# Units 22 and 23 of a top-k attention plus MLP kernel: transposed on TensorE and weighed one step sooner

## The chip, the core and the metric

The kernel runs on one NeuronCore of one Trainium2 chip, in one launch. The metric is device time in microseconds. Three runs of the kernel before took 1432.84, 1432.95 and 1433.07 us, so its median is 1432.95 us. A further execution was taken with the hardware profiler, and all rows below come from it.

## The reference

An attention over the 32 best keys of each query is followed by a two-layer perceptron with a leaky ReLU. All inputs are float32.

```python
B, H, S, D = 8, 8, 576, 64
scores = (q @ k.transpose(0, 1, 3, 2)) / sqrt(D)
kth = np.partition(scores, -32, axis=-1)[..., -32:-31]
scores = np.where(scores >= kth, scores, -1e9)
attn = exp(scores - max(scores)); attn /= sum(attn) + 1e-9
x = (attn @ v).transpose(0, 2, 1, 3).reshape(4608, 512)
h = x @ w_in                      # 512 -> 2048
out = np.maximum(0.01 * h, h) @ w_out   # 2048 -> 512
```

## The kernel before, in words

**Units and steps.** Heads are taken two at a time. A unit is 128 score rows for each of two heads, that is a block of 128 queries of one pair of heads, or the two 64-query remainders of two pairs. There are 144 units, and the kernel works on one unit per step. Steps come in pairs, written out by hand in `even(s)` (L729) and `odd(s, ...)` (L781); the order of the instructions on every engine is the order of this text, and each engine runs its own queue strictly in that order. In step s three units are in work: `cur` is unit s, `old` is unit s-1, `older` is unit s-2.

**The path of one unit.**

- The scores come from TensorE (`scores`, L237) into PSUM tiles `wide` and `narrow`, for two units at a time at the end of an even step; ScalarE copies them to `s_sb` (L246) in the odd step that follows. The tag `wide` has two buffers.
- In its own step, VectorE finds the 32 largest of each row (`top_k`): two TENSOR_TENSOR on the two halves of the row (L270), then rounds of MAX8 (L276) and MATCH_REPLACE8 (L281).
- One step later, ScalarE takes the negated limit (`limits`, L291), masks (L297), takes exponents with their sums (L300) and adds the small constant (L305, tile `ze`). GpSimd prepares the bias of the exponent (L292, L293).
- VectorE takes the reciprocal of `ze` (L309, tile `rz`). This happens only in even steps: for `older` after the two L270, and for `old` ahead of the last two MAX8. ScalarE then normalizes (L312).
- The weights must be turned before they can be multiplied with the values. The usual way is `split` and `transpose`: GpSimd copies the high and the low 16 bits apart (L321, two copies), SyncE writes them to DRAM (L322, two DMAs) and then starts a transposing DMA that brings them back as `wT` (L326).
- TensorE multiplies `wT` with the values (`weigh_whole`, L365) into a `wide` tile, and ScalarE copies the product to `x` (`keep_values`, L388).

**The hasty way.** Units 142 and 143, the last two, go another way. `transpose_in_haste` (L328) turns the nine 128-column blocks of `s_sb` with nine TensorE transposes (L336), into two `wide` tiles; `keep_transposed` (L339) copies these to `wT` on ScalarE with two copies (L342, 1024 and 128 columns). No GpSimd copy and no DMA is used. In the even step the two L342 stand after the exponents of `old`. In the odd step, L800 to L807 put these in a row: the transposes of `older`, the exponents of `old`, the two L342, and then at once the weighing of both units and its L388.

```python
    HASTY = (142, 143)                                  # L635
    def values_at(n):                                   # step in which unit n is weighed
        return (n | 1) + (2 if n in HASTY else 3)
```

**The MLP between the steps.** Tokens are cut in chunks: four of 128 tokens (chunks 0 to 3, `plain`), then sixteen of 256 (chunks 4 to 19, the rest of `mlp`). A chunk becomes ready when its last unit is weighed (`attended`, L654, in odd steps), and the MLP is a generator, of which `mlp_steps(budget)` runs a few matmuls at seven places of each step. For the big chunks `slot_budget` (L660) spreads the work of a chunk over the steps up to the next one's readiness; during the small chunks the budget is `EARLY_SHARE`, times 0.6 in a step whose `older` is hasty. The MLP's first layer is 8 groups of 8 matmuls (L504); `keep_hidden` (L492) then applies the leaky ReLU on ScalarE, one instruction for each group. This instruction is not written at once: it goes to a list `due`, and `catch_up` writes it at the next of a few fixed places, one of which lies between the masks of `old` and the normalization of `older` in every even step. The second layer is L518 (and L596 for the small chunks), its output is copied by L526 (or L588).

**Sums on GpSimd.** The second layer of the big chunks uses sums of weights and of hidden parts, which GpSimd makes with TENSOR_TENSOR (L443). They wait in a list, and `sum_now(2)` writes two of them in an even step, `sum_now(3)` three in an odd one. The generator of chunk 4 adds two sums of `w_out` (128x1024) of its own when it starts (`sum_last_weights`, L466).

**Which units end chunk 4.** Units 16 to 19 are the 64-query remainders of batches 0 and 1, units 20 to 23 the first whole blocks of batch 1; the last tokens of chunk 4 come from units 22 and 23.

Of the kernel before, what the change touches and what calls it, by code (L numbers as in the profile page):

```python
# [20 lines left out]
def kernel(  # L21
# [241 lines left out]
    def top_k(u):  # L263

        u.tops = small.tile([P, 2, ROUNDS, 8], F32, name="tops")
        pairs = work.tile([P, 2, 2, HS], F32, name="pairs", bufs=1)
        for n, op in enumerate((ALU.max, ALU.min)):
            nc.vector.tensor_tensor(pairs[:, :, n, :], u.both[:, :, 0:HS], u.both[:, :, HS:S], op)  # L270
        yield
        for r in range(ROUNDS):
            rest = [pairs[:, i, 0, :] if r < ROUNDS // 2 else
                    pairs[:, i, :, :].rearrange("p n h -> p (n h)") for i in range(2)]
            for i in range(2):
                nc.vector.max(out=u.tops[:, i, r, :], in_=rest[i])  # L276
            if r == ROUNDS - 2:
                yield
            if r + 1 < ROUNDS:
                for i in range(2):  # L280
                    nc.vector.match_replace(out=rest[i], in_to_replace=u.tops[:, i, r, :],  # L281
                                            in_values=rest[i], imm_value=LOWEST)
            yield
# [348 lines left out]

    HASTY = (142, 143)  # L635

    def values_at(n):

        return (n | 1) + (2 if n in HASTY else 3)

    steps = units

    def unit(n):
        return steps[n] if FIRST <= n < len(steps) else None
# [15 lines left out]
    def slot_budget(s):  # L660

        after = [at for at, _ in ready_at if at > s]
        if len(after) >= len(CHUNKS) - EARLY:
            return EARLY_SHARE * (0.6 if s - 2 in HASTY else 1.0)
        until = after[0] if after else s + 1
# [7 lines left out]
    with tc.manual_schedule():  # L673
# [55 lines left out]
        def even(s):  # L729
            cur, old, older = unit(s), unit(s - 1), unit(s - 2)  # L730
            in_haste = s - 2 in HASTY
            new = [u for u in steps[s + 2:s + 4] if u]
# [48 lines left out]
        def odd(s, new, ps, weighed):  # L781
            cur, old, older = unit(s), unit(s - 1), unit(s - 2)
            in_haste = s - 2 in HASTY
            picks = top_k(cur) if cur else iter(())
# [210 lines left out]
```

## Time and profile before

| what | value |
| --- | --- |
| median of the runs | 1432.95 us (1432.84 to 1433.07) |
| profiled execution, its own time | 1433.87 us |
| its span, first to last instruction | 1431.8 us |
| TensorE matmul busy | 1347.2 us, 94% |
| VectorE busy | 1319.2 us, 92% |
| ScalarE busy | 1023.0 us, 71% |
| GpSimd busy | 709.8 us, 50% |
| TensorE clock, mean of what was granted | 0.979 |

Shares over the whole span hide the stages: a stage is read from its own window. "PEclk" is the granted TensorE clock, 1.00 being full speed. In a timeline row the columns are the start, the duration of the row's instructions together, the engine, the line, the operation, output and input tiles, shapes, the count, and in brackets the idle time ahead of it with what ended it. Every float32 matmul shows as two rows' worth of instructions, so "x16" of L504 is eight matmuls. In step order, VectorE's L270 mark where steps begin: 287.98 us (step 24), 297.80 (25), 306.58 (26), 315.45 (27), 324.23 (28), 333.10 (29).

### The profile page before, as it was taken

How to read it: one execution, taken by the hardware profiler on the slowest of the kernel's cores; microseconds unless marked ns; L12 is line 12 of the kernel's file. 1: busy time of each engine (PE TensorE's matmuls, PEld its weight loads, DVE VectorE, ACT ScalarE, POOL GpSimd, SP SyncE). 2: the span in 40 equal slices, each digit the busy share in tenths (PEclk: the TensorE clock that was granted, in tenths of full speed). 3: DMA queues.
4: the chain of work that ended last, by engine and by line, in shares of the span. 5: the costliest groups of instructions: out<-in, count | busy, mean ns of one | idle time of the engine just before them, and what ended most of it. 6: DMA issues, size and time to landing. Idle time of an engine off the chain costs nothing.

```text
span 1431.8 us, 27705 instructions
## 1 busy us (share of the span) xinstructions
PE 1347.2 (94%) x9794; PEld 1031.4 (72%) x9794; DVE 1319.2 (92%) x3412; ACT 1023.0 (71%) x2144; POOL 709.8 (50%) x796
## 2 busy tenths in 40 slices
PE   6679599969999999999999999999999999999998
PEld 2234354447778888878888888888878888888887
DVE  7989999899999999999999999999999999999700
ACT  6866767677777777777777777777777777777621
POOL 2332373335555555555555555555555555555512
PEclk9889899989999999999999999999999999999999
DMA  7772545655666556756666556655676565655400
GB/s 291 250 222 67 140 134 172 193 141 133 165 185 174 144 144 186 196 152 139 177 175 173 141 164 174 186 142 155 175 182 168 141 157 142 169 145 136 125 12 15
DMA packets 399388, 224.91 MB, mean 157 GB/s; under 512 B 339216, under 2 KB 348432, under 8 KB 397328
## 3 DMA queue, kind: packets, MB, share of 16 engines
q1 hardware_dynamic: 398096, 222.08, 56.9%
q8 instruction: 77, 1.26, 0.4%
q10 hardware_dynamic: 1152, 1.05, 0.2%
q14 instruction: 63, 0.52, 0.1%
HBM read 46.14 MB, written 93.19 MB: 97 GB/s over the span
## 4 chain that ended last, share of the span: by engine, by line
DVE 70%; PE 18%; issue 6%; ACT 4%; DMA 1%; POOL 0%; DVEq 0%; POOLq 0%; ACTq 0%
DVE tops L276 34%; DVE pairs L281 26%; DVE pairs L270 7%; PE ph L504 4%; PE pz L518 4%; PE ph L405 3%; PE pz L596 2%; PE wide L365 2%; DMA raw<-in_weights_dram 1%; DVE rz L309 1%; PE wide L237 1%; ACT s_sb L300 1%; ACT s_sb L312 1%; DVE w_in L158 1%; PE narrow L237 0%
## 5 line engine op out<-in xcount | busy, mean ns | idle before, releaser
L276 DVE MAX8 tops<-pairs 128x8 f32<-128x288 f32 (+1 forms) x1152 | 636.3, 592 | 0.3 <-DVE rz L309 0.3
L504 PE MATMUL ph<-x,w_in 128*128 128x256 f32 x2048 | 457.5, 382 | 4.7 <-ACT gT L492 4.4
L281 DVE MATCH_REPLACE8 pairs<-tops,pairs 128x288 f32<-128x288 f32 (+1 forms) x864 | 460.6, 539 | 0.0
L504 PEld LDWEIGHTS ph<-x,w_in 128*128 128x128 f32 x2048 | 384.3, 190 | 84.0 <-issue 16.5
L321 POOL COPY split<-s_sb 128x1152 uint16<-128x1152 uint16 x284 | 316.8, 1144 | 186.1 <-ACT s_sb L312 186.1
L312 ACT ACTIVATE s_sb<-s_sb,rz 128x576 f32<-128x576 f32 x288 | 207.1, 766 | 151.6 <-DVE rz L309 151.5
L292 POOL TENSOR_TENSOR nbias<-tops 128x2 f32<-128x2 f32 x144 | 70.2, 488 | 401.5 <-DVE tops L276 398.0
L518 PE MATMUL pz<-w_out,gT 128*128 128x256 f32 x1024 | 226.5, 379 | 0.0
L270 DVE TENSOR_TENSOR pairs<-s_sb 128x576 f32<-128x576 f32 x288 | 212.8, 778 | 12.1 <-ACT s_sb L261 2.4
L300 ACT ACTIVATE s_sb<-s_sb,nbias 128x576 f32<-128x576 f32 x288 | 223.9, 785 | 0.0
L518 PEld LDWEIGHTS pz<-w_out,gT 128*128 128x128 f32 x1024 | 194.5, 190 | 26.6 <-issue 0.2
L297 ACT ACTIVATE s_sb<-s_sb,nleast 128x576 f32<-128x576 f32 x288 | 207.6, 768 | 4.7
L365 PE MATMUL wide<-wT,vt 128*64 128x128 f32 (+1 forms) x2560 | 156.4, 284 | 27.0 <-DMA wT<-apart 26.1
L365 PEld LDWEIGHTS wide<-wT,vt 128*64 128x64 f32 (+1 forms) x2560 | 128.3, 138 | 64.4 <-issue 34.0
L518 PE MATMUL pz<-raw,top 128*128 128x256 f32 x512 | 117.3, 384 | 4.6 <-ACT o_sb L526 4.4
L518 PEld LDWEIGHTS pz<-raw,top 128*128 128x128 f32 x512 | 95.2, 190 | 28.0 <-issue 8.0
L237 PE MATMUL wide<-kt,qt 64*64 64x352 f32 x1136 | 110.2, 458 | 0.0
L246 ACT COPY s_sb<-wide 128x704 f32<-128x704 f32 x142 | 108.0, 761 | 1.7 <-PE wide L237 1.7
L492 ACT ACTIVATE gT<-ph 128x512 f32<-128x512 f32 x128 | 75.3, 588 | 29.5 <-PE ph L504 29.5
L293 POOL TENSOR_SCALAR nbias<-nbias 128x2 f32<-128x2 f32 x144 | 84.7, 588 | 12.6
L291 ACT ACTIVATE nleast<-tops 128x2 f32<-128x2 f32 x144 | 28.6, 198 | 86.4 <-DVE tops L276 85.6
L526 ACT COPY o_sb<-pz 128x256 f32<-128x256 f32 x112 | 41.8, 374 | 60.8 <-PE pz L518 60.4
(70 smaller groups left out, 1238.4 us busy)
## 6 DMA issues: line engine op xcount, KB each, us to landing
apart<-split SPq DMA_DIRECT2D x284, 288.0 KB, 2.1
raw<-in_weights_dram SPq DMA_DIRECT2D x15, 1024.0 KB, 5.3
vt<-in_vk_dram SPq DMA_DIRECT2D x32, 320.0 KB, 3.8
qt<-in_qT_dram SPq DMA_DIRECT2D x32, 288.0 KB, 3.5
kt<-in_kT_dram SPq DMA_DIRECT2D x32, 288.0 KB, 3.6
out_dram<-o_sb SPq DMA_DIRECT2D x64, 128.0 KB, 2.2
wT<-apart SPq DMA_TRANSPOSE x142, 4.6
raw<-in_weights_dram SPq DMA_DIRECT2D x2, 512.0 KB, 4.3
```

The lines of the kernel that those rows point to most:

```text
L237: nc.tensor.matmul(to[r0:r0 + LEFT, i, :], qt[d, q0:q0 + LEFT], kt[d, k0:k1], start=True, stop=True)
L246: nc.scalar.copy(u.both[:, :, k0:k1], to)
L270: nc.vector.tensor_tensor(pairs[:, :, n, :], u.both[:, :, 0:HS], u.both[:, :, HS:S], op)
L276: nc.vector.max(out=u.tops[:, i, r, :], in_=rest[i])
L281: nc.vector.match_replace(out=rest[i], in_to_replace=u.tops[:, i, r, :], in_values=rest[i], imm_value=LOWEST)
L297: nc.scalar.activation(u.s[i], u.s[i], AF.Prelu, bias=u.nleast[:, i:i + 1], scale=1.0, alpha=BELOW)
L300: nc.scalar.activation(u.s[i], u.s[i], AF.Exp, bias=u.nbias[:, i:i + 1], scale=SCALE, accum_out=u.z[:, i:i + 1])
L312: nc.scalar.activation(u.s[i], u.s[i], AF.Copy, bias=0.0, scale=u.rz[:, i:i + 1])
L321: nc.gpsimd.tensor_copy(split, pairs[:, :, h])
L365: nc.tensor.matmul(po[n * D:(n + 1) * D, side, 0:P], v_of[u.pairs[0]][k, at, side, :], u.wT[k, at + side * NKC if at + 1 < NKC else at, :] ...
L504: nc.tensor.matmul(ph[:, i, 0:n], w_in[c][:, f * P:(f + 1) * P], x[:, c, 0:n], start=(c == 0), stop=(c == HP - 1),)
L518: nc.tensor.matmul(to, g[:, f, :], w(f), start=(first and f == 0), stop=(f == HALF - 1), skip_group_check=not first)
```

## The change

Units 22 and 23 join the list of units that are transposed in haste. No other text is changed.

```diff
-    HASTY = (142, 143)
+    HASTY = (22, 23, 142, 143)
```

Through `values_at`, both units are weighed in step 25, where it was step 26, and chunk 4 becomes ready in step 25 where it was step 27; `slot_budget` then spreads its MLP over ten steps where it was eight. In steps 24 and 25, `split` and `transpose` of the two units are left out and `transpose_in_haste` and `keep_transposed` come in; in step 25 the exponents of unit 24 move ahead of the MLP steps, as L800 to L807 have it. The order of the instructions on each engine follows from the text. On TensorE, from step 24 on, it is now: six of chunk 3's last eight L596, nine L336 (unit 22), the other two L596, L365 (units 20, 21), the scores of units 26 and 27, nine L336 (unit 23), L365 (units 22, 23), three groups of L504 of chunk 4, the scores of units 28 and 29. On ScalarE, after the exponents of unit 24 in step 25, it is now: two L342 (unit 23), L388 (units 22, 23), L492 of the first group, L291 and two L297 (unit 25, step 26), L492 of the second group, two L312 (unit 24), the exponents of unit 25 with L305. On GpSimd the two L443 on `w_out` follow the split of unit 24 in step 26, where they followed the split of unit 26 in step 28. VectorE's order is the same in both kernels.

## Prediction

> **What bounds the kernel now.** I read the chain of waits first, then the windows around steps 24 to 28, then the timelines there, then the same hasty pattern at the end of the trace.
>
> The page's shares of the chain, and the chain in time (start us, us, what) where it leaves VectorE for the last time:
>
> ```profile
> DVE 70%; PE 18%; issue 6%; ACT 4%; DMA 1%; POOL 0%; DVEq 0%; POOLq 0%; ACTq 0%
> ```
> ```profile
> 1260.71 0.21 ACT nleast L291
> ...
> 1265.53 0.49 ACT gT L492
> 1266.03 0.04 issue
> 1266.07 1.99 PE ph L504 x8
> ```
>
> From 290 to 1260.7 us the chain is VectorE's alone; after that TensorE runs on to the end. TensorE is full in most windows there, but it follows: asked for 296 to 1340 us, the wait view names no wait of VectorE at all. So a stall put into VectorE at 314 us reaches the end in full, and idle time taken from TensorE there does not.
>
> Windows at the place of the change (first column the stretch, then its length, PE, PEld, DVE, ACT, POOL busy, granted clock):
>
> ```profile
> 293.46:296.88 3.42, 3.42 (x59) 2.62 (x62) 3.42 (x9) 2.08 (x7) 1.63 (x2) 1.00 0.58 210
> 296.88:300.29 3.41, 1.14 (x20) 0.45 (x12) 3.38 (x8) 3.38 (x7) 2.35 (x3) 1.00 0.15 47
> 300.29:303.70 3.41, 0.00 (x0) 0.00 (x0) 3.41 (x13) 3.35 (x9) 1.18 (x2) 0.50 1.02 236
> ```
>
> TensorE idles, waiting for the transposing DMAs of units 22 and 23 (6.04 and 5.39 us, the wait view of TensorE), and its clock falls to half. VectorE stays full.
>
> **The change, part by part.**
>
> Taken away: four L321 (4.46 us of GpSimd), four DMAs, two transposing DMAs. Nobody but L365 waited for them; SyncE's later loads and output writes move up, and none of them was late. Worth nothing. TensorE's 11.4 us of waiting go too, worth nothing while VectorE sets the end.
>
> Step 24. Unit 22's nine transposes take 1.4 us (rows at 1358 and 1370 us: 1.43 and 1.20), between L312 at 292.8 and the last two L596, which end at 295.3. The two L342 take 1.18 us on ScalarE after L305, to 295.7; L588 and its output DMAs (1.51 us in the trace) follow, and L312 of unit 23 starts at 297.2 where it started at 296.48. ScalarE is then 0.7 us late; the scores of 26 and 27 end at 299.7 and are there in time for L246; L305 of unit 24 is done at 304.3 for a reciprocal at 307.96. Free.
>
> Step 25 is where it costs. Rows that size it, from the end of the trace where units 142 and 143 do the same, and from steps 26 to 28:
>
> ```profile
> 1371.65 1.18 ACT L342 COPY wT<-wide 128x1024 f32<-128x1024 f32 x2 [0.62 <-PE wide L336]
> 1372.71 2.35 PE L365 MATMUL wide<-wT,vt 128*64 128x128 f32 x40 [0.99 <-ACT wT L342]
> 1378.74 0.60 ACT L492 ACTIVATE gT<-ph 128x512 f32<-128x512 f32 x1 [2.97 <-PE ph L504]
> ```
> ```profile
> 311.14 0.20 ACT L305 ACTIVATE ze<-z 128x2 f32<-128x2 f32 x1
> 325.74 0.58 ACT L492 ACTIVATE gT<-ph 128x512 f32<-128x512 f32 x1
> 326.22 1.43 ACT L312 ACTIVATE s_sb<-s_sb,rz 128x576 f32<-128x576 f32 x2
> 329.20 0.20 ACT L305 ACTIVATE ze<-z 128x2 f32<-128x2 f32 x1
> ```
> ```profile
> 313.95 0.15 DVE L309 RECIPROCAL rz<-ze 128x2 f32<-128x2 f32 x1
> ```
>
> ScalarE's L342 of unit 23 starts at 304.3 and gives L365 leave at 305.35. From L365's start to L492 of the first group the end of the trace shows 1378.74 - 1372.71 = 6.03 us, so L492 runs at 311.4. Behind it in ScalarE's queue stand L291 and L297 of unit 25, ready since 306.5; they end by 313.2. Then comes L492 of the second group, which needs 16 more rows of L504 at 0.2205 us (12.35 us for 56): 305.35 + 6.03 + 3.53 = 314.9. Only behind it stand L312 of unit 24 and the exponents of unit 25. In step 28 the way from such an L492 to the start of L305 takes 329.20 - 325.74 = 3.46 us, and from there to VectorE's L309 0.24 us (289.69 to 289.93). L309 of unit 25 so comes at 318.6 at full clock, where VectorE reaches it at 313.95 (L305 was done at 311.3, 2.6 us of slack). Stall: **4.65 us**. Before, no L492 stood in step 26; from step 28 on the groups were ready before ScalarE asked. Now the first group starts only after a transpose, a copy and a weighing, and its two L492 are in the queue already.
>
> The clock comes on top. TensorE is idle from 299.8 to 301.1 and from 302.7 to 305.35. The trace's window with 1.14 of 3.41 us busy was followed by half clock; at 102 us one with 1.22 lost the clock, at 95 us one with 1.66 kept it, and at 160 us it came back after one with 2.88. By these rows, put at any phase over the idle stretch, the clock falls between 302 and 306 us and returns between 308 and 311, costing L365 and the two groups 1.3 to 3.0 us. I take **2.1**, the middle over phases (2.6 by this trace's phase). Bounds: 0 if it does not fall, 3.0.
>
> The Trainium skill ("TensorE: Matmul & The Clock Gate", What's actually happening) has the clock halved after at least one idle window of about 3.4 us. The longest gap here is shorter, so read strictly the clock would hold and the sum would lack these 2.1 us; the trace's window with a third of it busy says otherwise, and I follow the trace.
>
> Then the shared stretch with GpSimd:
>
> ```profile
> 327.71 2.23 POOL L321 COPY split<-s_sb 128x1152 uint16<-128x1152 uint16 x2 [2.63 <-ACT s_sb L312]
> 329.91 4.70 POOL L443 TENSOR_TENSOR w_out<-w_out,w_out 128x1024 f32<-128x1024 f32 x2
> ...
> 333.10 2.80 DVE L270 TENSOR_TENSOR pairs<-s_sb 128x576 f32<-128x576 f32 x2
> ```
> ```profile
> 1342.63 2.66 DVE L270 TENSOR_TENSOR pairs<-s_sb 128x576 f32<-128x576 f32 x2
> 1343.00 1.67 POOL L443 TENSOR_TENSOR top<-top,gT 128x512 f32<-128x512 f32 x1
> ```
>
> An L270 that meets an L443 waits until that one is over: 2.80 us where two L270 take 1.46. At 1343 us they alternate, each L270 behind one L443 (2.66 us with L443 of 1.28). Now the two L443 on w_out come behind unit 24's split. Call t the start of the second L492 (317.0 with the clock's loss). By the rows above, L443 run from t + 4.17 (329.91 - 325.74) for 2.36 us each; VectorE's L309 is at t + 3.70, two MAX8 later L270 of unit 27 at t + 5.2. Its first waits 1.3 us for the first L443; the second L443 takes the turn; the second L270 waits 2.3 us for it. Cost **3.6 us** (bounds: 0 if they miss, 3.75 with both in full), whatever t is, because both sides hang on the same L312. The old meeting at 333.10 is gone: **-1.34 us**.
>
> Behind that nothing is late: L300 of unit 26 waits about 1.5 us for its bias (GpSimd is behind its L443), but its reciprocal is wanted only 8 us later; the transposing DMA of unit 25 lands some 3 us into step 28, two steps ahead of need.
>
> Chunk 4's MLP is spread thinner. That saves TensorE's time only, and before the scores of step 132 TensorE's order has the same count of MLP matmuls to within four.
>
> Sum: 4.65 + 2.1 + 3.6 - 1.34 = **+9.0 us**. The profiled execution (1433.87 us, of which 1431.8 is span) would become 1442.9; the median before is 0.92 lower, so I give 1432.95 + 9.0 = 1442.0.
>
> **The rivals.**
>
> *TensorE is the bound after all: faster.* It is 18.00 of 18 us busy in many windows. If it never again waited for VectorE between 316 and 1266 us, its 11.4 us of DMA waits and 1.9 us of half clock (38 L365 in 4.14 us, 40 in 2.35) would come off, less 2.6 us of transposes: 10.7 us, 1422.3. It decides if VectorE's stall is made good later. For: the chain ends on TensorE. Against: the absent VectorE waits for a thousand us; a lag of TensorE would show there. Chance 0.05.
>
> *The stall is absorbed: the same.* If the second L492 comes no later than 313.95 - 3.70 = 310.25 us, L309 does not wait, and what is left is the meeting, moved or gone: -1.3 to +2.3 us, 1431.6 to 1435.2. It needs that L492 some 5 us sooner than even the sum at full clock has it. Chance 0.08.
>
> *The stall alone, clock kept, L443 missed:* 4.65 - 1.34 = +3.3, 1436.3. Chance 0.15.
>
> *The main case,* with clock and meeting: +7.2 to +9.9, 1440.1 to 1442.9. Chance 0.72. A further L443 (1.27 us each) meeting an L270 in the shifted steps 28 to 34 could add up to 2.5: 1445.4.
>
> **How the numbers follow.** About 0.2%, 2.9 us, is what a measurement of this kernel can tell from no change. Slower than that are the main case and the stall alone: 0.72 + 0.15 = 0.87; within it the absorbed one, 0.08; faster 0.05. The range leaves out the last two and goes from the stall alone to a further meeting: 1436 to 1445.5.
>
> **What would show it.** VectorE's wait view should have one new wait of L309 for L305 of 5.9 to 7.7 us at about 314, then a pair of L270 of about 5 us, and L270 at 333 back at 1.46 or so. ScalarE should wait for L504 ahead of both L492. TensorE's waits on the transposing DMA at 304 and 310 should be gone, its clock at half for one or two windows of 3.4 us after 302. If VectorE has no wait at 314 the stall is wrong; if it has it and the time is unchanged, the bound is.

## The result, and the profile after

The changed kernel takes 1441.8 us in the median of six runs (1440.68 to 1444.04), beside 1433.01 us for the kernel before on the same chip (1431.65 to 1433.99): a ratio of 1.0064 with a 95% interval of 1.0051 to 1.0077, 8.8 us more. Its profiled execution took 1443.57 us, of which 1441.5 is span.

The shares of its chain, and the chain of waits (start us, us, what) where it leaves VectorE for the last time:

```profile
DVE 75%; PE 12%; issue 6%; ACT 4%; DMA 1%; POOL 0%; DVEq 0%; POOLq 0%
```
```profile
1296.16 0.03 issue
1296.19 1.44 ACT s_sb L312 x2
```

The chain still ends on TensorE, but it stays on VectorE longer than before, to 1296.16 us. The wait view of VectorE from 304 to 1330 us, empty before, has one line (total us, times, longest):

```profile
DVE rz L309 <- ACT ze L305: 6.9, 1, 6.9
```

VectorE's timeline around it (start, us of the row, what, and in brackets the idle time ahead of it):

```profile
322.15 0.17 DVE L309 RECIPROCAL rz<-ze 128x2 f32<-128x2 f32 x1 [6.86 <-ACT ze L305]
323.67 4.78 DVE L270 TENSOR_TENSOR pairs<-s_sb 128x576 f32<-128x576 f32 x2
335.80 1.46 DVE L270 TENSOR_TENSOR pairs<-s_sb 128x576 f32<-128x576 f32 x2
344.67 1.43 DVE L270 TENSOR_TENSOR pairs<-s_sb 128x576 f32<-128x576 f32 x2
```

The rows are L309 of unit 25, and the L270 of units 27, 28 and 29. First the stall, then a pair of L270 that takes 4.78 us instead of 1.43. The pair of unit 29, which took 2.80 us before at 333.10, is back at 1.43.

ScalarE's timeline shows why L305 came late, and TensorE's why ScalarE did:

```profile
310.93 0.37 ACT L388 COPY x<-wide 128x256 f32<-128x256 f32 x1 [4.30 <-PE wide L365]
315.00 0.60 ACT L492 ACTIVATE gT<-ph 128x512 f32<-128x512 f32 x1 [3.70 <-PE ph L504]
318.45 0.60 ACT L492 ACTIVATE gT<-ph 128x512 f32<-128x512 f32 x1 [1.29 <-PE ph L504]
318.94 1.43 ACT L312 ACTIVATE s_sb<-s_sb,rz 128x576 f32<-128x576 f32 x2
321.92 0.20 ACT L305 ACTIVATE ze<-z 128x2 f32<-128x2 f32 x1
```
```profile
306.51 4.32 PE L365 MATMUL wide<-wT,vt 128*64 128x128 f32 x40 [2.33 <-ACT wT L342]
337.98 3.31 PE L365 MATMUL wide<-wT,vt 128*64 128x128 f32 x38 [2.66 <-DMA wT<-apart]
```

ScalarE waits three times for TensorE, and the masks, L312, the exponents and L305 stand behind. L365 takes 4.32 us for 40 rows that take 2.35 at full clock. In the windows there (stretch, length, then PE, PEld, DVE, ACT and POOL busy, granted clock) the clock is at half for 6.82 us:

```profile
301.50:304.93 3.43, 1.42 (x9) 0.99 (x9) 3.43 (x12) 3.43 (x8) 0.00 (x0) 1.00 0.00 0
304.93:308.34 3.41, 1.83 (x18) 1.83 (x20) 3.31 (x8) 1.67 (x5) 0.41 (x2) 0.50 0.00 0
308.34:311.75 3.41, 3.41 (x28) 2.60 (x25) 3.41 (x13) 0.37 (x1) 0.38 (x1) 0.50 0.00 0
311.75:315.17 3.42, 3.42 (x17) 3.01 (x16) 3.42 (x9) 0.17 (x1) 0.00 (x0) 1.00 0.02 5
```

On GpSimd the two sums of `w_out` (L443) come behind unit 24's split and run into the L270 of unit 27:

```profile
320.43 2.23 POOL L321 COPY split<-s_sb 128x1152 uint16<-128x1152 uint16 x2 [11.72 <-ACT s_sb L312]
322.63 5.20 POOL L443 TENSOR_TENSOR w_out<-w_out,w_out 128x1024 f32<-128x1024 f32 x2
```

Where the time went is read best from VectorE's step starts, since its order is the same in both kernels. The table compares the start of each L270 with the trace of before.

| L270 of unit | before, us | after, us | later by, us | added since the row above |
| --- | --- | --- | --- | --- |
| 26 | 306.58 | 307.86 | 1.28 | |
| 27 | 315.45 | 323.67 | 8.22 | +6.94, the stall at L309 |
| 28 | 324.23 | 335.80 | 11.57 | +3.35, the new meeting with L443 |
| 29 | 333.10 | 344.67 | 11.57 | 0 |
| 30 | 343.25 | 353.45 | 10.20 | -1.37, the old meeting gone |
| 35 | 387.40 | 397.59 | 10.19 | -0.01 |

The 1.28 us were there ahead of step 24, where both kernels have the same order; they are a difference between two executions. (In the four kernels of the first experiments, which have the same order up to there, VectorE reaches unit 26 at 304.73 to 306.77 us.) From unit 26 to unit 35 the change costs 6.94 + 3.35 - 1.37 - 0.01 = 8.91 us. The shift then stays between 10.18 and 10.23 us up to unit 142. From unit 35 to the end of the span it takes 1044.4 us before and 1044.0 after: 0.4 us of the 8.91 come back, all of them between units 142 and 143.

### The profile page after: what moved, and what is told of

The parts are those of the page before. It is cut to its first block, busy times and chain, and to the rows that moved or that the text cites. A ratio compares the mean times of both kernels' runs of the same rounds, so it can differ in the third digit from the quotient of the medians.

```text
span 1441.5 us, 27729 instructions
## 1 busy us (share of the span) xinstructions
PE 1356.2 (94%) x9812; PEld 1037.1 (72%) x9812; DVE 1321.4 (92%) x3412; ACT 1026.4 (71%) x2148; POOL 705.6 (49%) x792
## 4 chain that ended last, share of the span: by engine, by line
DVE 75%; PE 12%; issue 6%; ACT 4%; DMA 1%; POOL 0%; DVEq 0%; POOLq 0%
DVE tops L276 36%; DVE pairs L281 28%; DVE pairs L270 8%; PE ph L504 4%; PE pz L518 3%; PE ph L405 1%; PE wide L365 1%; DMA raw<-in_weights_dram 1%; DVE rz L309 1%; ACT s_sb L312 1%; ACT s_sb L300 1%; ACT s_sb L246 1%; DVE w_in L158 1%; PE pz L596 0%; PE wide L237 0%
## 5 line engine op out<-in xcount | busy, mean ns | idle before, releaser
L504 PE MATMUL ph<-x,w_in 128*128 128x256 f32 x2048 | 459.3, 383 | 6.1 <-ACT gT L492 3.8
L504 PEld LDWEIGHTS ph<-x,w_in 128*128 128x128 f32 x2048 | 385.9, 191 | 85.3 <-issue 16.3
L321 POOL COPY split<-s_sb 128x1152 uint16<-128x1152 uint16 x280 | 312.4, 1144 | 189.0 <-ACT s_sb L312 189.0
L312 ACT ACTIVATE s_sb<-s_sb,rz 128x576 f32<-128x576 f32 x288 | 207.2, 767 | 153.3 <-DVE rz L309 152.8
L270 DVE TENSOR_TENSOR pairs<-s_sb 128x576 f32<-128x576 f32 x288 | 214.8, 786 | 12.4 <-ACT s_sb L261 2.7
L297 ACT ACTIVATE s_sb<-s_sb,nleast 128x576 f32<-128x576 f32 x288 | 207.8, 769 | 4.7
L365 PE MATMUL wide<-wT,vt 128*64 128x128 f32 (+1 forms) x2560 | 159.5, 287 | 21.0 <-DMA wT<-apart 17.5
L365 PEld LDWEIGHTS wide<-wT,vt 128*64 128x64 f32 (+1 forms) x2560 | 130.3, 140 | 58.7 <-issue 33.6
L492 ACT ACTIVATE gT<-ph 128x512 f32<-128x512 f32 x128 | 75.5, 590 | 35.0 <-PE ph L504 35.0
L291 ACT ACTIVATE nleast<-tops 128x2 f32<-128x2 f32 x144 | 28.6, 198 | 86.6 <-DVE tops L276 85.5
```

The costliest lines, as they stand in the source:

```text
L297: nc.scalar.activation(u.s[i], u.s[i], AF.Prelu, bias=u.nleast[:, i:i + 1], scale=1.0, alpha=BELOW)
L312: nc.scalar.activation(u.s[i], u.s[i], AF.Copy, bias=0.0, scale=u.rz[:, i:i + 1])
L321: nc.gpsimd.tensor_copy(split, pairs[:, :, h])
L365: nc.tensor.matmul(po[n * D:(n + 1) * D, side, 0:P], v_of[u.pairs[0]][k, at, side, :], u.wT[k, at + side * NKC if at + 1 < NKC else at, :] ...
L504: nc.tensor.matmul(ph[:, i, 0:n], w_in[c][:, f * P:(f + 1) * P], x[:, c, 0:n], start=(c == 0), stop=(c == HP - 1),)
```

## Experiments

The theory: VectorE loses 8.9 us in three places. (1) Two L492 of chunk 4, and the L388 ahead of them, stand in ScalarE's queue before the exponents that VectorE waits for. (2) TensorE's clock is at half while it works for them. (3) The two L443 on `w_out` meet an L270 pair. The rivals: the transposes and the copies L342 cost something themselves; the early weighing alone makes the stall; the stall covers the meeting, so that taking one away leaves the other; the end is set by TensorE, which starts chunk 4 late or early.

In what follows, "net shift" is the time from VectorE's L270 of unit 26 to that of unit 35, less the 80.82 us of before. Each net shift is read from one profiled execution; kernels that should agree do so within 0.1 us. Medians stand beside the kernel before in the same set of runs. They hold what executions differ by ahead of step 24, and the net shift does not.

| kernel | net shift, us | median, before beside it | ratio, 95% interval |
| --- | --- | --- | --- |
| after | +8.91 | 1441.8, 1433.01 | 1.0064 (1.0051 to 1.0077) |
| weighed later | +0.01 | 1433.35, 1433.14 | 0.9999 (0.9991 to 1.0008) |
| MLP later | +0.77 | 1434.97, 1433.14 | 1.0010 (1.0002 to 1.0019) |
| sums later | +5.68 | 1438.54, 1433.14 | 1.0042 (1.0028 to 1.0056) |
| L492 behind | +2.21 | 1434.36, 1433.14 | 1.0011 (1.0003 to 1.0020) |
| after, plain DMA | +9.00 | 1440.60, 1432.91 | 1.0055 (1.0043 to 1.0067) |
| the same, TensorE busy | +7.63 | 1437.51, 1432.91 | 1.0028 (1.0017 to 1.0039) |
| the same, L492 behind, sums later | +0.27 | 1431.15, 1432.91 | 0.9990 (0.9980 to 1.0001) |
| before, plain DMA | +0.03 | 1431.43, 1433.15 | 0.9990 (0.9981 to 0.9999) |
| the same, sums apart | -1.37 | 1429.79, 1432.91 | 0.9981 (0.9972 to 0.9989) |
| after, plain DMA, all three | -1.38 | 1429.96, 1433.15 | 0.9981 (0.9973 to 0.9990) |

**Transposed on TensorE, weighed at the old time.** Only the weighing of units 22 and 23 goes back to step 26, and with it chunk 4 to step 27.

```diff
-        return (n | 1) + (2 if n in HASTY else 3)
+        return (n | 1) + (2 if n in (142, 143) else 3)
```

> The changed kernel, but units 22 and 23 are weighed in step 26 and chunk 4 is ready in step 27, as in the kernel before; the transposes on TensorE and the two pairs of copies stay. Theory (the cost is the queue of step 25 and 26: the early weighing and the two L492 ahead of unit 25's exponents, and GpSimd's two L443 that then meet L270): no new wait of VectorE after step 24, the old meeting of L270 with L443 in step 29 is back at 1.3 us; time as the kernel before, within 0.5 us. Rival (the transposes and copies themselves cost the time, 2.6 us of TensorE and 2.3 us of ScalarE): 2 to 5 us slower than before.

The net shift is +0.01 us. From 300 to 1330 us VectorE waits for nothing. TensorE's clock fell here too:

```profile
305.42 4.32 PE L365 MATMUL wide<-wT,vt 128*64 128x128 f32 x40 [2.33 <-ACT wT L342]
```

It is the weighing of units 22 and 23 again: TensorE has nothing else to do and comes to it at the same time. But its L388 now stands a step later in ScalarE's queue, at 317.23 us, behind L305 of unit 25 at 311.32, and nobody waits. So the eighteen transposes, the four L342, the splits and DMAs left out, and the half clock by itself cost nothing. What costs comes with the early weighing and the early chunk 4, which the next experiments take apart.

**Weighed early, the MLP of chunk 4 at its old time.** The early weighing alone; `EARLY` is 4.

```diff
-            ready_at.append(((values_at(n) | 1) if n >= FIRST else FIRST - 1, ch))
+            ready_at.append(((values_at(n) | 1) + 2 * (ch == EARLY) if n >= FIRST else FIRST - 1, ch))
```

> The changed kernel with the early weighing kept, but chunk 4 is ready in step 27 as before, so that no L492 stands in step 26. Theory: what is left is the first L388, on which ScalarE waits for a weighing at half clock; it ends at about 311.3 us of the changed kernel's trace, and from there L291, L297, L312, L300 and L305 take 4.6 us, so that L309 of unit 25 waits about 0.8 us (none at full clock) where it waited 6.9; L443 is back behind unit 26's split. Time 0.8 us slower than before (0 to 1.5). Rival (the early weighing is what costs, MLP or not): 6 to 9 us slower than before.

VectorE's wait for unit 25 is still there, but it is small:

```profile
307.98 0.37 ACT L388 COPY x<-wide 128x256 f32<-128x256 f32 x1 [4.29 <-PE wide L365]
313.05 0.17 DVE L309 RECIPROCAL rz<-ze 128x2 f32<-128x2 f32 x1 [0.69 <-ACT ze L305]
```

ScalarE's L388 waits 4.29 us for the weighing at half clock, and that uses up the 2.6 us of slack and 0.69 us more. The early weighing is thus worth +0.77 us, and the two L492 with the early sums make up the other 8.1 of the 8.91.

**The sums of `w_out` one step later.** GpSimd writes no sums in step 26.

```diff
-            sum_now(2)
+            if s != 26:
+                sum_now(2)
```

> The changed kernel, but no sum is written in step 26, so that GpSimd's two L443 on w_out come one step later, behind unit 25's split. Theory: the wait of L309 stays at 6.9 us (5.9 to 7.7 with the clock's phase), the two L270 of unit 27 are back at 1.45 us, no L270 meets L443 in steps 27 to 29: 6.9 - 1.4 = 5.5 us slower than before, 3.4 us faster than the changed kernel. Rival (the meeting is covered by the wait, or moves to the next L270): 8 to 9 us slower than before, as the changed kernel.

```profile
319.13 0.17 DVE L309 RECIPROCAL rz<-ze 128x2 f32<-128x2 f32 x1 [6.96 <-ACT ze L305]
320.65 1.43 DVE L270 TENSOR_TENSOR pairs<-s_sb 128x576 f32<-128x576 f32 x2
```

The stall stays and the pair is back at 1.43 us: net +5.68, which is 3.23 less than the changed kernel. The meeting is paid on top of the stall, not covered by it.

**The two L492 behind the exponents.** ScalarE's copies for the MLP are held back from step 25's weighing until the exponents of unit 25 are written in step 26.

```diff
     def catch_up():
-        while due:
+        while due and not held[0]:
...
-            mlp_steps(budget)
+            if s != 26:
+                mlp_steps(budget)
...
                 sums(old)
+            if held[0]:
+                held[0] = False
+                catch_up()
...
                 keep(values(s, []))
+                held[0] = s == 25
```

> The changed kernel with TensorE's order around the place as it is, but the two L492 of the first two groups are written behind the exponents of unit 25 in ScalarE's queue (the MLP steps skip one place in step 26 for it). Theory: L309 of unit 25 waits about 0.8 us, only for the first L388; the split of unit 24 comes earlier with it, and the two L443 meet the two L270 of unit 27 as in the changed kernel, 3.6 us. 0.8 + 3.6 - 1.4 = 3.0 us slower than before (2 to 4). Rival (TensorE's late start holds the scores or something else, not the place of L492): wait of 4 us or more, 7 us slower or more.

```profile
312.96 0.17 DVE L309 RECIPROCAL rz<-ze 128x2 f32<-128x2 f32 x1 [0.16 <-ACT ze L305]
314.48 4.76 DVE L270 TENSOR_TENSOR pairs<-s_sb 128x576 f32<-128x576 f32 x2
```

The wait falls from 6.86 to 0.16 us and the meeting remains: net +2.21, inside the 2 to 4 that were expected. The medians differ by 1.2 us only, below that range: less the 0.4 us that come back at the end, the net shift stands for 1.8 us, which the interval (0.4 to 2.9 us) covers. In the profiled execution the clock was at half for one window only, so that L365 took 3.80 us; a part of what L388 could have cost is missing for that reason.

**The same kernels with another DMA.** In the kernels from here on, the transposing DMA is replaced by a plain DMA of the same bytes throughout. They leave out the turning of the weights and their low halves, and only their times are used. Two controls show what that does by itself.

```diff
-            nc.gpsimd.tensor_copy(split, pairs[:, :, h])
+            nc.gpsimd.tensor_copy(split, pairs[:, :, 1])
...
-        nc.sync.dma_start_transpose(out=u.wT.bitcast(U16), in_=u.apart.rearrange("p h n -> (p h) n"))
+        nc.sync.dma_start(u.wT.rearrange("p c n -> p (c n)").bitcast(U16), u.apart.rearrange("p h n -> p (h n)"))
```

The changed kernel with it:

> The changed kernel with a plain DMA in the place of each transposing one, as a base for the three that follow. Left out: the turning of the weights, and their low halves, since GpSimd copies the high half both times; the same count of bytes goes out and comes back, and the order on TensorE, VectorE, ScalarE and GpSimd is the changed kernel's. Theory: nothing of the loss hangs on the transposing DMAs, so L309 of unit 25 waits 6 to 7.7 us, the two L270 of unit 27 take 4.8 us together, and from step 26 to step 35 VectorE takes 8 to 9.5 us more than in the kernel before; time 7 to 10 us above the kernel before. Rival (the way of the transposing DMAs is part of it): a loss of VectorE there under 6 us.

The kernel before with it:

> The kernel before with plain DMAs in the place of the transposing ones (weights not turned, low halves left out): the base of the plain set. Theory: VectorE has no wait after step 24 and its pair of L270 in step 29 takes 2.80 us, so from step 26 to 35 it takes what the kernel before takes, to 0.1 us; the time differs from the kernel before only by what the faster return of the weights does ahead of step 24, 0 to 3 us less. Rival (the plain DMAs change the stretch): a difference there of over 0.5 us.

The net shifts are +9.00 and +0.03 us, where the originals have +8.91 and 0. The stall (6.93 us) and the meeting (4.77) are the same. The kind of DMA has no part in the loss. The second control is 1.7 us faster than the kernel before in the median; that this lies ahead of step 24 is not shown, for VectorE reaches unit 26 at 304.49 us there, hardly below the 304.73 to 307.86 of the kernels with the transposing DMA, and at 307.12 in the first control.

**TensorE kept busy.** To the changed kernel with the plain DMA, matmuls that nobody reads are added: one of 128x512 behind the scores in step 24, two behind the transposes in step 25. They fill the gap that lost the clock.

```diff
+        def keep_busy(count):
+            pw = ps_ml.tile([P, 512], F32, name="pw", tag="ml")
+            for _ in range(count):
+                nc.tensor.matmul(pw, ident, w_in[0][:, 0:512], start=True, stop=True)
...
+            if s == 24:
+                keep_busy(1)
...
+                if s == 25:
+                    keep_busy(2)
```

> As the plain copy of the changed kernel (weights not turned, low halves left out), with three more float32 matmuls of 128x512 whose product nobody reads, one behind the scores of units 26 and 27 and two behind the transposes of unit 23, so that TensorE is not idle for more than about half a microsecond ahead of the weighing. Theory: the clock stays at full over 300 to 320 us, the weighing takes 2.35 us where it took 4.32 in the changed kernel, L309 of unit 25 waits 4.3 to 4.9 us where it waited 6.9; the L270 of unit 27 still meet both L443 (3.35 us). From step 26 to 35 VectorE loses 4.6 + 3.35 - 1.37 = 6.6 us on the kernel before. Rival (the half clock is not what lengthens the wait): wait 6.5 us or more.

```profile
294.06 1.50 ACTq L589 DMA_DIRECT2D out_dram<-o_sb  x1
303.74 2.35 PE L365 MATMUL wide<-wT,vt 128*64 128x128 f32 x40 [0.61 <-ACT wT L342]
313.23 0.60 ACT L492 ACTIVATE gT<-ph 128x512 f32<-128x512 f32 x1 [1.29 <-PE ph L504]
316.94 0.17 DVE L309 RECIPROCAL rz<-ze 128x2 f32<-128x2 f32 x1 [5.56 <-ACT ze L305]
```

L365 runs at full clock. From its start to the second L492 it takes 9.49 us (303.74 to 313.23), where the changed kernel took 11.94 (306.51 to 318.45) and its copy with the plain DMA 12.02: the half clock is worth 2.45 to 2.53 us. VectorE's wait, 5.56 us, lies above the 4.3 to 4.9 that were expected, and the net shift, 7.63, above 6.6. In this profiled execution one output DMA of ScalarE (L589) took 1.50 us to issue, where the others take 0.34, ahead of everything in step 25; without these 1.16 us the wait would have been 4.40. That figure is worked out, not measured. The kernel with all three edits, below, bears it out: it has the same three matmuls and no slow issue, and its L365 starts 1.35 us ahead of VectorE's L270 of unit 26, as in the changed kernel and its copy, where here it starts 0.20 ahead. So the matmuls that nobody reads don't delay the weighing, and 1.15 us of the wait belong to the slow issue. 4.40 and 2.45 make 6.85, the 6.86 of the changed kernel.

**L492 behind and sums later, together.** Both edits above, with the plain DMA.

> As the plain copy of the changed kernel (weights not turned, low halves left out), with both L492 behind the exponents of unit 25 and no sum written in step 26. Theory: L309 of unit 25 waits 0 to 0.8 us by the clock's phase, no L270 between steps 26 and 30 meets an L443 of GpSimd, and the old meeting of 1.37 us is gone too: from step 26 to 35 VectorE gains 0.5 to 1.4 us on the kernel before, and the time is some 9 us below the plain copy of the changed kernel. Rival (something else of the change costs besides these two): VectorE loses 1 us or more there.

```profile
312.45 0.17 DVE L309 RECIPROCAL rz<-ze 128x2 f32<-128x2 f32 x1 [0.68 <-ACT ze L305]
322.75 2.32 DVE L270 TENSOR_TENSOR pairs<-s_sb 128x576 f32<-128x576 f32 x2
```

A gain of 0.5 to 1.4 us was expected; the net is +0.27. What was overlooked: moved one step, with the stall gone, the second of the two L443 (319.10 to 323.79 us together) meets the L270 of unit 28, 2.32 us instead of 1.46. The wait of 0.68, this meeting's 0.87 and the old meeting's -1.37 make 0.18 of the 0.27. The loss is undone, but one meeting was only moved.

**The kernel before, its sums one per step.** No change at all to units 22 and 23, only the meeting at 333.10 taken away.

```diff
-            sum_now(2)
+            sum_now(1 if s == 28 else 2)
...
-            sum_now(3)
+            sum_now(2 if s == 29 else 3)
```

> The kernel before with plain DMAs in the place of the transposing ones (weights not turned, low halves left out), and with one of the two sums on w_out written in step 28 and the other in step 29. Theory: the pair of L270 in step 29 takes 1.45 us where it took 2.80 and nothing else moves there: from step 26 to 35 VectorE gains 1.35 us on the kernel before. Rival (the meeting was covered, or comes back at the next L270): no gain there.

```profile
329.62 1.43 DVE L270 TENSOR_TENSOR pairs<-s_sb 128x576 f32<-128x576 f32 x2
```

Net -1.37 us, the size of the old meeting.

**All three mended in the changed kernel.** TensorE busy, L492 behind, and the sums of `w_out` one in step 27 and one in step 28.

```diff
-            sum_now(2)
+            if s != 26:
+                sum_now(1 if s == 28 else 2)
...
-            sum_now(3)
+            sum_now(1 if s == 27 else 3)
```

> As the plain copy of the changed kernel (weights not turned, low halves left out), with three changes at once: TensorE kept busy by three unread matmuls of 128x512, both L492 behind the exponents of unit 25, and the two sums on w_out written one in step 27 and one in step 28. Theory: L309 of unit 25 waits 0 to 0.3 us, no L270 meets an L443 between steps 26 and 30: VectorE gains 1.1 to 1.4 us from step 26 to 35 on the kernel before, as the kernel before with its sums apart does; starting chunk 4 sooner is worth nothing more. Rival (the early start pays once the stall is gone): a gain of 3 us or more, there or behind it.

```profile
311.85 0.15 DVE L309 RECIPROCAL rz<-ze 128x2 f32<-128x2 f32 x1
330.99 1.43 DVE L270 TENSOR_TENSOR pairs<-s_sb 128x576 f32<-128x576 f32 x2
```

No wait, no meeting, net -1.38 us: the same as the kernel before with its sums apart (-1.37), and the medians, 1429.96 and 1429.79, don't differ by more than their intervals. So the change, with all its costs removed, brings nothing up to unit 142. What it gives TensorE, an earlier weighing and an earlier chunk 4, is not what VectorE was short of there. The 0.4 us at the end come back here as well, too little for the medians to tell. These two were the fastest tried. Of their distance to the kernel before (ratio 0.9981), the plain DMA has about half (0.9990 in its control) and the old meeting the rest. Since the plain DMA doesn't turn the weights, only the spread sums could be carried over, and with the transposing DMA they were not tried.

## Why the prediction was right

- **VectorE sets the end, and a stall reaches it in full.** Right. The shift of 10.2 us holds for a thousand microseconds. The rival in which TensorE is the bound fell: TensorE's 11.4 us of DMA waits at 304 and 310 went, and no time came off.
- **The queue on ScalarE.** The order and the walk held. Less the 1.28 us by which this execution came late, L365 started at 305.23 (forecast 305.35), the second L492 at 317.17 (317.0), L309 at 320.87 (318.6 + 2.1 = 320.7). The full clock's part is 4.40 us by the busy experiment (5.56 measured, less the 1.16 of the slow issue), where the forecast had 4.65.
- **The clock.** The forecast took 2.1 us, inside 1.3 to 3.0, and mentioned 2.6 by the trace's phase; 2.45 was measured, in the phase that this execution had. The Trainium skill ("TensorE: Matmul & The Clock Gate", What's actually happening) names an idle window of about 3.4 us for the fall. The prediction counted the nine transposes as work, by which the longest gap is 2.33 us in the trace of after, and concluded that by the skill the clock would hold. Whether transposes count is not shown. The 1.42 us that TensorE was busy in the window ahead of the fall are transposes alone (L336, one row each, where a float32 matmul shows as two), and without them TensorE has nothing from 301.07 to 306.51 us; no run separates the two readings. What does differ from an idle window are windows partly busy with ordinary matmuls: the one of before that the prediction went by (1.14 of 3.41 us, scores), and this one after the change, filled in its last third by the late weighing of units 24 and 25. Half clock followed both; there the measurement stands.

```profile
335.64:339.05 3.41, 1.07 (x20) 1.08 (x22) 3.31 (x11) 3.29 (x6) 0.79 (x2) 1.00 0.59 124
339.05:342.46 3.41, 3.41 (x36) 2.40 (x34) 3.41 (x11) 1.90 (x6) 3.17 (x3) 0.50 0.27 99
```

- **The meeting.** Forecast 3.6 us, measured 3.35. The places were right to 0.02 us (from the second L492, L443 begins 4.18 us later and the L270 pair 5.22, forecast 4.17 and 5.2), and so was the alternation; but the turns overlap a little, and the second L443 is over at 327.83, where two of 2.36 us and one L270 of 0.72 between them would end at 328.07. The old meeting was sized at 1.34 and measured at 1.37.
- **What was called free** was free: the experiment that keeps the transposes and copies but weighs later shifts nothing.
- **Small errors.** The bias was waited for by 0.84 us where 1.5 was forecast. The transposing DMA of unit 25 was said to land two steps ahead of need; TensorE waited 2.66 us for it at 337.98 and its clock fell for one more window. That step of the reading was wrong. It cost nothing, since the shift of VectorE's step starts from unit 30 to 142 moves by no more than 0.05 us. The 0.4 us that come back at the end were not foreseen. The kernel before has the same pattern once more in step 142: L492 waits 2.85 us for L504 at 1335.83 us ahead of the exponents, and VectorE's L309 waits 2.31 us for them at 1341.11. In every kernel whose chunk 4 starts early that wait of L309 is 1.87 to 1.89 us, in the others 2.31 to 2.33. Why it is shorter stays open.

The sum was forecast as 9.0 us, and the terms as measured give 4.40 + 2.45 + 3.35 - 1.37 = 8.83, near the net shift of 8.91. With the 0.4 us at the end the trace has 8.5 us, and the medians 8.8 (7.3 to 11.0 by the interval). That 9.0 lies so close is in part luck: the stall and the meeting were forecast 0.25 us too large each, the clock 0.35 too small, the end not at all.

## What to carry to other kernels

Giving an engine that follows its work sooner gained almost nothing here, and cost 8.8 us: the copies that empty its results enter another engine's queue sooner, and the small, urgent instruction that stands behind them waits for the whole chain ahead. Before moving work, write down what stands behind each moved instruction on its queue and who is next to wait. And look at every instruction that moves along, the sums on GpSimd here: their meeting cost 3.35 of the 8.91 us, and it is no part of the stall.

## What the runs showed of the hardware

TensorE's clock fell after windows that were partly busy with ordinary matmuls: 1.14 of 3.41 us (before, at 296.88) and 1.07 of 3.41 (after, at 335.64). After 1.66 of 3.41 (before, at 95.49) it held. The windows ahead of the weighing of units 22 and 23 (1.42 of 3.43 us in the changed kernel, 1.06 of 3.40 with the L492 behind) were busy with transposes alone; half clock followed them for two windows and for one. The same gap with three unread matmuls in it kept full clock.

Two L270 beside two L443 alternate, one of each in turn: 4.78 us instead of 1.43 for the pair, and 5.20 instead of 4.70 for the L443. The first L443 takes 2.37 us and the first L270 1.94, ending 0.6 us after it; the second ones are

```profile
324.95 2.88 POOL L443 TENSOR_TENSOR w_out<-w_out,w_out 128x1024 f32<-128x1024 f32 x1
325.54 2.91 DVE L270 TENSOR_TENSOR pairs<-s_sb 128x576 f32<-128x576 f32 x1
```

The two MAX8 that ran beside the first L443 at 322.24 took 1.40 us, as elsewhere. The Trainium skill ("SBUF — State Buffer", SBUF: two separate sides) describes a port pair of VectorE and GpSimd that goes to whichever operation starts first, for its whole length, where the VectorE operation has two SBUF inputs and the GpSimd one reads SBUF. L270 takes two halves of a row in SBUF, and L443 reads `w_out` there; these rows agree with it.

A single output DMA on ScalarE's queue took 1.50 us to issue instead of 0.34. It was seen once, and its cause stays open.
